# Windowed attention ahead of two mixture-of-experts layers: order of exponential and transpositions, layout of v, quarters of the array

## The chip, the cores and the metric

The kernel runs on one core of a Trainium2 chip. The metric is device microseconds of one execution. Beside the plain executions there is one taken with the profiler; its time and its span are given below.

## What is computed

Attention over q, k and v of shape (4, 8, 576, 64) with a window of 32 keys: heads 0 to 3 look at the last 32 positions, heads 4 to 7 at every fourth of the last 128. Its output, 2304 rows of 512, goes through a layer that assigns each row to one of 8 experts, with a capacity, and then through one that mixes two experts for each row.

```python
rel = pos[:, None] - pos[None, :]
mask_plain = (rel >= 0) & (rel < 32)
mask_dil = (rel >= 0) & (rel < 128) & (rel % 4 == 0)
scores = np.where(masks, scale * np.matmul(q, k.transpose(0, 1, 3, 2)), -1e9)
attn = np.exp(scores - scores.max(-1, keepdims=True))
x = np.matmul(attn / (attn.sum(-1, keepdims=True) + 1e-9), v)
x = moe(x)    # each row to one expert of 8, capacity N // 8
out = moe2(x) # two experts for each row, softmax over the two
```

## The kernel before

All data are float32. The host reorders the positions of the dilated heads so that they too become a plain window; then every block of 64 queries needs 96 keys. A group g is a batch and half of its heads (four heads, as two pairs i of two heads h); there are eight groups, and each is cut into a unit of five blocks and one of four, so 16 units u. Even groups hold the plain heads, odd groups the dilated ones.

For a unit, `scores` (L237) multiplies each block's queries with its 96 keys: 64 rows of the array for head h, 64 columns, output s in PSUM; VectorE scales and masks (L251) into p and takes the maximum (L256); GpSimd subtracts it (L257). `norm` (L259) has ScalarE take the exponential (L262), VectorE sum it (L264), add 1e-9 (L265) and invert (L266), and GpSimd multiply (L267). `flip` (L269) transposes p on TensorE (L278), four blocks to a PSUM tile ps, of which there are two, and ScalarE copies each tile out (sb, L280): three tiles for a unit of five blocks (4, 4 and 2 transpositions), two for one of four. `pv` (L286) multiplies with v (L297), and ScalarE copies the output o to x (L302, L308).

Each engine carries out its instructions in the order in which the program issues them. The loop at the end of `attention` issues for unit u: `flip(u)`, `norm(u + 2)`, `scores(u + 4)`, `pv(u)`; behind an even group come `gate` and `logits` of the batch before. So while a unit is transposed, VectorE and GpSimd work on later ones. Tiles of p are six, of s and o two each, of q, k and v four groups.

SP issues all loads on one queue, in the order of the calls of `load` (L217: q, k, and for the first two groups a half of the mask) and `load_v` (L226), with the constants ct and ct2 in between; groups 4 to 7 are issued as units finish. An issue waits until the DMA that last used its semaphore has landed; eight semaphores are used in turn. `consts2` (L176) makes small tables on GpSimd out of ct and ct2, issued behind the scores of unit 3. `warm` (L361) keeps TensorE busy with matmuls on zeros at the start. Attention ends with `steps` (L338, at 100.55 us in the trace) and the routing of the first expert layer follows.

Of the kernel before, what the change touches and what calls it, by code (L numbers as in the profile page):

```python
# [9 lines left out]
F32 = mybir.dt.float32  # L10
# [13 lines left out]
NT = N // 128  # L24
# [34 lines left out]
for _n, _w in (("ident", 128), ("iota", 128), ("prio", E), ("iota8", E),  # L59
               ("ge", 3 * NT), ("ge2", 5 * NCOL), ("pos", NCOL), ("ovf", (N - CAP2) // 128),  # L60
               ("tri", 128), ("shift", (len(DIGITS) + len(DIGITS_FIX)) * NT), ("tri1", 128), ("tokcp", NT * 2), ("colp", NCOL * 2)):
    if _n == "tri":
        _WK = _W
    _C[_n] = (_W, _w)
    _W += _w


def _constants():
# [8 lines left out]
    put("ident", np.eye(128))  # L77
    put("tri", (p[:, None] < p[None, :]))
    put("iota", p)
# [36 lines left out]
def prep(inputs):  # L116
# [10 lines left out]
    y[:, :, 4:] = x[:, :, 4:].reshape(B, 144, 4, 4, D).transpose(0, 2, 1, 3, 4).reshape(B, S, 4, D)  # L127
    a["v"] = y.reshape(B, S, DM)
    g = np.zeros((4, 128, 32), np.float32)
# [16 lines left out]
class Body:  # L146
# [29 lines left out]
    def consts2(self):  # L176
        nc, c, cp = self.nc, self.c, self.cp
        self.tri = cp.tile([128, 128], BF, name="tri")
        nc.gpsimd.tensor_copy(self.tri, c("tri"))
        self.ones = cp.tile([128, 128], BF, name="ones")  # L180
        nc.gpsimd.memset(self.ones, 1.0)
        self.iotab = cp.tile([128, 128], BF, name="iotab")
        nc.gpsimd.tensor_copy(self.iotab, c("iota"))
        self.c256 = cp.tile([128, 128], BF, name="c256")
        nc.gpsimd.memset(self.c256, 256.0)
        self.shift = cp.tile([128, self.nr, NT], I32, name="shift")
        o = 0 if self.exact else len(DIGITS) * NT
        nc.gpsimd.tensor_copy(self.shift.rearrange("p r c -> p (r c)"), c("shift")[:, o:o + self.nr * NT])
        self.tri1 = cp.tile([128, 128], BF, name="tri1")
        nc.gpsimd.tensor_copy(self.tri1, c("tri1"))  # L190
        self.prio = cp.tile([128, E], BF, name="prio")
        nc.gpsimd.tensor_copy(self.prio, c("prio"))
        self.tokcp = cp.tile([128, NT, 2], BF, name="tokcp")
        nc.gpsimd.tensor_copy(self.tokcp.rearrange("p c v -> p (c v)"), c("tokcp"))
        self.pt4 = self.st.tile([GB, NCOL, 4], BF, name="pt4")
        nc.gpsimd.tensor_copy(self.pt4[:, :, 0:2], c("colp", GB).rearrange("p (c v) -> p c v", v=2))
        self.L = self.st.tile([128, NT, E], F32, name="L")
        self.unit = self.st.tile([128, 1], F32, name="unit")


    def attention(self, x0T):
        nc, tc, A = self.nc, self.tc, self.A
        with ExitStack() as ctx:
# [22 lines left out]
            def load_v(g):  # L226
                b, t = divmod(g, 2)
                VT[g] = vp.tile([KW, NB, 256], F32, name="vt")
                v = A["v"]
                nc.sync.dma_start(VT[g][:, 0, :], v[b, 0:KW, 256 * t:256 * t + 256])  # L230
                nc.sync.dma_start(VT[g][:, 1:NB, :],
                                  bass.AP(tensor=v.tensor, offset=v.offset + (b * S + 32) * DM + 256 * t,
                                          ap=[[DM, KW], [64 * DM, NB - 1], [1, 256]]))

            groups = [(g, j0, n) for g in range(2 * B) for j0, n in (CUTS if g == 0 else ((0, 5), (5, 4)))]

            def scores(u):  # L237
                g, j0, n = groups[u]
                s = pS.tile([128, 2, 512], F32, name="s")
                for i in range(2):  # L240
                    for jj in range(n):
                        j = j0 + jj
                        w = _win(j)
                        for h in range(2):
                            r = slice(64 * h, 64 * h + 64)
                            nc.tensor.matmul(s[r, i, jj * KW:(jj + 1) * KW], QT[g][r, i, 64 * j:64 * j + 64],  # L246
                                             KT[g][r, i, w:w + KW], start=True, stop=True)
# [21 lines left out]
            def flip(u):  # L269
# [4 lines left out]
                while q < 2 * n:  # L274
# [8 lines left out]
                    q += m  # L283
                return blk

            def pv(u, blk):  # L286
                g, j0, n = groups[u]
                b, t = divmod(g, 2)
                for i in range(2):
                    o = pO.tile([128, 512], F32, name="o")  # L290
                    for jj in range(n):
                        sb, a = blk[i * n + jj]
                        j = j0 + jj
                        for h in range(2):
                            r = slice(64 * h, 64 * h + 64)
                            hh = 2 * i + h
                            nc.tensor.matmul(o[r, jj * 64:(jj + 1) * 64], VT[g][:, j, hh * 64:hh * 64 + 64],  # L297
                                             sb[:, a, r], start=True, stop=True)
                    dst = x0T[2 * t + i][:, b * S:(b + 1) * S]
# [77 lines left out]
            load_v(3)  # L377
            nu = len(groups)
            scores(0)
            scores(1)  # L380
# [4 lines left out]
            scores(3)  # L385
            self.consts2()
            warm(WARM[2])
            for u, (g, j0, n) in enumerate(groups):
                if j0 == 0 and g + 4 < 2 * B:
                    load(g + 4)  # L390
                    load_v(g + 4)
                blk = flip(u)
                if u + 2 < nu:
                    norm(u + 2)
                if u < len(WARM) - 3:
                    warm(WARM[3 + u])
                if u + 4 < nu:
                    scores(u + 4)
                pv(u, blk)
                if g and g % 2 == 0:  # L400
                    if j0 == 0:
# [1070 lines left out]
```

## Time and profile before

| | |
|---|---|
| median of three executions | 919.64 us (917.78 to 921.02) |
| profiled execution | 921.74 us |
| its span, first to last instruction | 919.9 us |
| TensorE busy | 851.6 us (93%) |
| VectorE busy | 517.9 us (56%) |
| ScalarE busy | 367.1 us (40%) |
| GpSimd busy | 183.8 us (20%) |
| instruction fetches (DMA queue q8) | 55 packets, 0.90 MB |

Busy time is that of the whole span, in which attention is the first ninth; what bounds that stretch is read from the stretch itself. PE is TensorE, DVE VectorE, ACT ScalarE, POOL GpSimd, SP SyncE; L12 is line 12 of the kernel before.

### The profile page before, as it was taken

Reading aid. Unit: us, or ns where it says so; the run is one execution under the profiler, and the core shown is the slowest. Engines: PE = TensorE matmul, PEld = TensorE weight load, DVE = VectorE, ACT = ScalarE, POOL = GpSimd, SP = SyncE. Lnnn points to the kernel's source line nnn. Section 1 sums busy time; section 2 is a strip of 40 time slices with the busy share of each in tenths; the row PEclk is TensorE's granted clock in tenths of the full one; section 3 lists DMA queues with packets and bytes.
Section 4 is the critical chain, followed back from the end, with each engine's and each line's share of the span. In section 5 each row is a group of like instructions: output and inputs, shape, how many; then the busy total and the mean of one; then the engine's idle time right before and its main releaser. Section 6 shows DMA issues by size and latency. Waiting matters only on the chain.

```text
span 919.9 us, 16944 instructions
## 1 busy us (share of the span) xinstructions
PE 851.6 (93%) x6723; PEld 772.8 (84%) x6725; DVE 517.9 (56%) x1540; ACT 367.1 (40%) x669; POOL 183.8 (20%) x155
## 2 busy tenths in 40 slices
PE   7789849889999999889898999999999999999993
PEld 5677738789988999789797989989899898998983
DVE  6557576779998643964855635427255272552300
ACT  2557643434334645545324334333343333432310
POOL 4646210110112100010023221221212212122011
PEclk9889969999999999999999999999999999999997
DMA  9962373436565765354335553544535445453012
GB/s 307 265 179 45 128 243 138 144 119 209 164 205 147 262 198 177 95 178 145 107 57 170 144 133 73 157 83 136 144 75 151 91 125 150 81 149 47 14 24 38
DMA packets 59641, 126.33 MB, mean 137 GB/s; under 512 B 7456, under 2 KB 14880, under 8 KB 59552
## 3 DMA queue, kind: packets, MB, share of 16 engines
q1 hardware_dynamic: 46080, 94.53, 33.0%
q0 software_dynamic: 10496, 25.77, 14.4%
q10 hardware_dynamic: 2976, 4.85, 1.7%
q8 instruction: 55, 0.90, 0.4%
q14 instruction: 34, 0.28, 0.1%
HBM read 100.49 MB, written 24.72 MB: 136 GB/s over the span
## 4 chain that ended last, share of the span: by engine, by line
PE 71%; DVE 13%; DMA 7%; ACT 4%; issue 3%; SPq 1%; POOL 1%; ACTq 0%; POOLq 0%; DVEq 0%
PE m L774 58%; DVE wlo L739 3%; PE s L246 2%; PE t L1048 2%; PE r L546 1%; DMA kt<-in_k_dram 1%; PE o L297 1%; DMA raw<-in_w2a_dram 1%; DMA g<-xr,idx 1%; DVE hl L762 1%; PE ps L278 1%; DVE R L683 1%; ACT whi L735 1%; DMA ct<-in_consts_dram 1%; PE t L434 1%
## 5 line engine op out<-in xcount | busy, mean ns | idle before, releaser
L774 PE MATMUL m<-xh,whi 128*128 128x384 f32 (+2 forms) x768 | 237.0, 309 | 0.6 <-DVE hl L762 0.6
L774 PE MATMUL m<-xl,whi 128*128 128x384 f32 (+2 forms) x768 | 236.1, 307 | 0.0
L774 PE MATMUL m<-xh,wlo 128*128 128x384 f32 (+2 forms) x768 | 235.9, 307 | 0.0
L739 DVE TENSOR_TENSOR wlo<-raw,whi 128x512 fp32r<-128x512 f32 x256 | 163.8, 684 | 52.2 <-ACT whi L735 51.9
L762 DVE SCALAR_TENSOR_TENSOR hl<-m,hh 128x256 fp32r<-128x256 f32 (+2 forms) x192 | 90.0, 476 | 151.5 <-ACT hh L761 135.2
L761 ACT ACTIVATE hh<-m 128x256 fp32r<-128x256 f32 (+2 forms) x192 | 81.3, 427 | 178.0 <-PE m L774 164.5
L774 PEld LDWEIGHTS m<-xl,whi 128*128 128x128 f32 x768 | 146.1, 190 | 4.7 <-issue 4.4
L735 ACT ACTIVATE whi<-raw 128x1024 fp32r<-128x1024 f32 x128 | 134.4, 1052 | 38.1 <-DMA raw<-in_w1a_dram 16.3
L774 PEld LDWEIGHTS m<-xh,whi 128*128 128x128 f32 x768 | 146.0, 190 | 1.2 <-DVE hl L762 0.8
L774 PEld LDWEIGHTS m<-xh,wlo 128*128 128x128 f32 x768 | 145.8, 190 | 0.5 <-issue 0.5
L774 PE MATMUL m<-whi,hl 128*128 128x512 f32 x320 | 129.0, 403 | 0.5 <-DVE hl L762 0.5
L774 PE MATMUL m<-wlo,hh 128*128 128x512 f32 x320 | 125.4, 392 | 0.0
L774 PE MATMUL m<-whi,hh 128*128 128x512 f32 x320 | 125.2, 391 | 0.0
L1085 POOL DMA_INDIRECT out_dram<-y,tk x40 | 64.1, 1604 | 278.7 <-ACT y L1084 264.5
L1084 ACT ACTIVATE y<-m,wte 128x512 f32<-128x512 f32 x40 | 27.5, 688 | 144.5 <-issue 93.9
L774 PE MATMUL m<-hh,whi 128*128 128x288 f32 x256 | 78.5, 307 | 3.6 <-DVE over L499 3.0
L758 DVE TENSOR_TENSOR xl<-t,xh 128x512 fp32r<-128x512 f32 (+1 forms) x72 | 41.8, 586 | 71.0 <-ACT xh L757 70.5
L774 PE MATMUL m<-hl,whi 128*128 128x288 f32 x256 | 79.3, 310 | 2.6 <-DVE hl L762 1.4
L774 PE MATMUL m<-hh,wlo 128*128 128x288 f32 x256 | 78.2, 306 | 0.0
L1034 POOL DMA_INDIRECT g<-x,pos x40 | 38.8, 970 | 177.9 <-issue 125.5
L774 PEld LDWEIGHTS m<-whi,hl 128*128 128x128 f32 x320 | 60.5, 189 | 12.5 <-DVE hl L762 1.4
L774 PEld LDWEIGHTS m<-wlo,hh 128*128 128x128 f32 x320 | 60.4, 189 | 12.6
(220 smaller groups left out, 1096.2 us busy)
## 6 DMA issues: line engine op xcount, KB each, us to landing
raw<-in_w1a_dram SPq DMA_DIRECT2D x32, 512.0 KB
raw<-in_w2a_dram SPq DMA_DIRECT2D x32, 512.0 KB
raw<-in_w1b_dram SPq DMA_DIRECT2D x32, 512.0 KB
raw<-in_w2b_dram SPq DMA_DIRECT2D x32, 512.0 KB
vt<-in_v_dram SPq DMA_DIRECT2D x8, 768.0 KB
qt<-in_q_dram SPq DMA_DIRECT2D x8, 576.0 KB
kt<-in_k_dram SPq DMA_DIRECT2D x8, 576.0 KB
xr<-g SPq DMA_DIRECT2D x18, 256.0 KB
```

What stands on the lines that cost most here:

```text
L246: nc.tensor.matmul(s[r, i, jj * KW:(jj + 1) * KW], QT[g][r, i, 64 * j:64 * j + 64], KT[g][r, i, w:w + KW], start=True, stop=True)
L278: nc.tensor.transpose(ps[:, a, :], p[:, q + a, :], self.ident)
L735: nc.scalar.activation(hi, raw, AF.Copy)
L739: self.pend.append((chunk, self.pe + LOW[0], lambda s=s: nc.vector.tensor_tensor(lo[:, s], raw[:, s], hi[:, s].bitcast(F32), op=OP.subtract)))
L758: self.nc.vector.tensor_tensor(xl, ps, xh.bitcast(F32), op=OP.subtract)
L761: self.nc.scalar.activation(hh, ps, AF.Relu)
L762: self.later(0.4, lambda: self.nc.vector.scalar_tensor_tensor(hl, ps, 0.0, hh.bitcast(F32), op0=OP.max, op1=OP.subtract))
L774: self.nc.tensor.matmul(ps, a, b, start=i == 0, stop=i == n - 1)
L1034: nc.gpsimd.indirect_dma_start(out=g[:, :DM], out_offset=None, in_=self.x1[:rows, :], in_offset=bass.IndirectOffsetOnAxis(ap=pos[:, b:b + ...
L1048: nc.tensor.transpose(ps[:, kk * 128:(kk + 1) * 128], g[:, kk * 128:(kk + 1) * 128], self.ident)
L1084: nc.scalar.activation(y, ps, AF.Copy, scale=wt[:, b:b + 1])
L1085: nc.gpsimd.indirect_dma_start(out=self.out, out_offset=bass.IndirectOffsetOnAxis(ap=tok[:, b:b + 1], axis=0), in_=y, in_offset=None, comp ...
```

## The change

Four things change. The scores' loop runs over block, pair i, head h, and the half of the output rows is h xor i, so that four matmuls in turn use all four combinations of row half and column half of the array; `pv` reads the halves accordingly. In the main loop `norm(u + 2)` is issued ahead of `flip(u)`, and `flip` hands back after its second tile, so that the third tile's transpositions stand behind `scores(u + 4)`. The host lays v out as [batch, half of heads, 64, 9 blocks, 256], so that a partition's eight blocks are one run of 8 KB, and `load_v` makes four DMAs of it instead of two. The unused table tri goes; `consts2` is issued ahead of the first scores, and five of its casts form `consts3`, issued behind `pv` of unit 6.

```diff
@@ load_v
-                v = A["v"]
-                nc.sync.dma_start(VT[g][:, 0, :], v[b, 0:KW, 256 * t:256 * t + 256])
-                nc.sync.dma_start(VT[g][:, 1:NB, :],
-                                  bass.AP(tensor=v.tensor, offset=v.offset + (b * S + 32) * DM + 256 * t,
-                                          ap=[[DM, KW], [64 * DM, NB - 1], [1, 256]]))
+                v = A["v"][b, t]
+                nc.sync.dma_start(VT[g][:64, 0, :], v[:, 0, :])
+                nc.sync.dma_start(VT[g][64:, 0, :], v[:KW - 64, 1, :])
+                nc.sync.dma_start(VT[g][KW - 64:, 1:, :], v[:, 1:, :])
+                nc.sync.dma_start(VT[g][:KW - 64, 1:, :], v[32:, :NB - 1, :])
@@ scores
-                for i in range(2):
-                    for jj in range(n):
-                        j = j0 + jj
-                        w = _win(j)
+                for jj in range(n):
+                    j = j0 + jj
+                    w = _win(j)
+                    for i in range(2):
                         for h in range(2):
                             r = slice(64 * h, 64 * h + 64)
-                            nc.tensor.matmul(s[r, i, jj * KW:(jj + 1) * KW], QT[g][r, i, 64 * j:64 * j + 64],
+                            nc.tensor.matmul(s[half(h ^ i), i, jj * KW:(jj + 1) * KW], QT[g][r, i, 64 * j:64 * j + 64],
                                              KT[g][r, i, w:w + KW], start=True, stop=True)
@@ flip
-                return blk
+                    yield blk
@@ pv
-                                             sb[:, a, r], start=True, stop=True)
+                                             sb[:, a, half(h ^ i)], start=True, stop=True)
@@ attention, ahead of the units
+            self.consts2()
             scores(0)
             scores(1)
             norm(0)
...
             scores(3)
-            self.consts2()
             warm(WARM[2])
             for u, (g, j0, n) in enumerate(groups):
...
-                blk = flip(u)
                 if u + 2 < nu:
                     norm(u + 2)
+
+                turn = flip(u)
+                next(turn)
+                blk = next(turn)
                 if u < len(WARM) - 3:
                     warm(WARM[3 + u])
                 if u + 4 < nu:
                     scores(u + 4)
+                for _ in turn:
+                    pass
                 pv(u, blk)
+                if u == 6:
+                    self.consts3()
```

On ScalarE, around unit 2, the program before has the two output copies of unit 1 (x_75, x_76), the three tile copies of unit 2 (sb), the exponential of unit 4 (p, 128x960) and the output copies of unit 2:

```order
L302 ACTIVATE x_75<-o 128x256
L302 ACTIVATE x_76<-o 128x256
L280 ACTIVATE sb<-ps 96x512 x2
L280 ACTIVATE sb<-ps 96x256
L262 ACTIVATE p<-p 128x960
L308 ACTIVATE x_77<-o 128x144 x2
```

The changed program has there:

```order
L307 ACTIVATE x_75<-o 128x256
L307 ACTIVATE x_76<-o 128x256
L267 ACTIVATE p<-p 128x960
L285 ACTIVATE sb<-ps 96x512 x2
L285 ACTIVATE sb<-ps 96x256
L313 ACTIVATE x_77<-o 128x144 x2
```

The exponential of unit 4 now stands ahead of the three copies of unit 2.

On GpSimd, at the start of the program, the first work on scores (p from p and the maxima mx) stands before right behind one memset:

```order
L325 MEMSET amo 128x128
L257 ISA
L257 TENSOR_TENSOR p<-p,mx 128x960
L257 TENSOR_TENSOR p<-p,mx 128x768
L267 TENSOR_TENSOR p<-p,su 128x960
```

And in the changed program:

```order
L330 MEMSET amo 128x128
L179 MEMSET ones 128x128
L181 CAST iotab<-ct 128x128
L183 MEMSET c_183 128x128
L262 ISA
L262 TENSOR_TENSOR p<-p,mx 128x960
L262 TENSOR_TENSOR p<-p,mx 128x768
```

Two memsets and a cast that reads ct, the constants that SP loads behind the first two groups' q, k and masks, have moved ahead of the first subtraction.

On SP, from the load of ct2 (ct_108) to q and k of group 3 (qt, kt), the program before issues v of groups 1 and 2 in two DMAs each:

```order
L373 DMA ct_108<-in_consts_dram 128x484
L230 DMA vt<-in_v_dram 96x256
L231 DMA vt<-in_v_dram 96x8x256
L230 DMA vt<-in_v_dram 96x256
L231 DMA vt<-in_v_dram 96x8x256
L220 DMA qt<-in_q_dram 128x2x576
L222 DMA kt<-in_k_dram 128x2x576
```

And the changed program:

```order
L378 DMA ct_108<-in_consts_dram 128x356
L231 DMA vt<-in_v_dram 64x256
L232 DMA vt<-in_v_dram 32x256
L233 DMA vt<-in_v_dram 64x2048
L234 DMA vt<-in_v_dram 32x2048
L231 DMA vt<-in_v_dram 64x256
L232 DMA vt<-in_v_dram 32x256
L233 DMA vt<-in_v_dram 64x2048
L234 DMA vt<-in_v_dram 32x2048
L221 DMA qt<-in_q_dram 128x2x576
L223 DMA kt<-in_k_dram 128x2x576
```

Each v is now four DMAs, two of them with runs of 2048 elements, and ct2 is narrower by the 128 columns of tri.

## Rows read from the trace of the kernel before

**Rows 1.** Windows of attention: stretch, length, each engine's busy us (instructions), clock, DMA

```profile
33.70:59.90 26.20, 21.14 (x335) 17.77 (x336) 12.72 (x20) 11.04 (x26) 11.86 (x8) 0.80 0.83 195
59.90:87.04 27.14, 26.07 (x509) 22.22 (x507) 19.42 (x29) 18.86 (x45) 17.20 (x11) 1.00 0.45 114
```

**Rows 2.** TensorE in order of time: start, length, work, count, idle before

```profile
33.71 1.87 PE L246 MATMUL s<-kt,qt 64*64 64x96 f32 x40 [2.54 <-DMA kt<-in_k_dram]
...
42.07 0.86 PE L297 MATMUL o<-sb,vt 96*64 96x64 f32 x18 [2.09 <-issue]
...
50.02 0.51 PE L278 MATMUL ps<-ct,p 128*96 128x128 f32 x3
53.35 1.30 PE L278 MATMUL ps<-ct,p 128*96 128x128 f32 x5 [2.83 <-issue]
```

**Rows 3.** DMA queues, 39 to 42 us (packets, MB, share of 16 engines)

```profile
q8 instruction: 1, 0.02, 2.8%
```

**Rows 4.** DMA queues, 50 to 52 us

```profile
q8 instruction: 1, 0.02, 4.0%
```

**Rows 5.** Busy time and granted clock after the two stops

```profile
42.07:46.00 3.93, 3.93 (x38) 3.08 (x39) 0.60 (x1) 2.92 (x8) 1.81 (x2) 0.57 1.07 258
53.35:59.90 6.55, 6.55 (x74) 5.83 (x75) 3.19 (x5) 2.68 (x5) 1.75 (x2) 0.52 0.10 36
```

**Rows 6.** VectorE in order of time, unit 6 to unit 8

```profile
64.67 1.09 DVE L251 SCALAR_TENSOR_TENSOR p<-s,mask 128x960 f32<-128x960 f32 x1
...
67.28 0.95 DVE L264 TENSOR_REDUCE su<-p 128x8 f32<-128x768 f32 x1 [0.26 <-ACT p L262]
68.27 0.71 DVE L265 TENSOR_SCALAR su<-su 128x8 f32<-128x8 f32 x1
...
69.14 0.91 DVE L251 SCALAR_TENSOR_TENSOR p<-s,mask 128x768 f32<-128x768 f32 x1
...
73.00 1.09 DVE L251 SCALAR_TENSOR_TENSOR p<-s,mask 128x960 f32<-128x960 f32 x1
```

**Rows 7.** GpSimd in order of time, the same stretch

```profile
67.16 1.79 POOL L257 TENSOR_TENSOR p<-p,mx 128x960 f32<-128x960 f32 x1 [0.48 <-DVE mx L256]
...
71.25 1.47 POOL L257 TENSOR_TENSOR p<-p,mx 128x768 f32<-128x768 f32 x1 [0.41 <-DVE mx L256]
```

**Rows 8.** VectorE in order of time, other units

```profile
15.48 1.11 DVE L251 SCALAR_TENSOR_TENSOR p<-s,mask 128x960 f32<-128x960 f32 x1
...
35.62 1.16 DVE L251 SCALAR_TENSOR_TENSOR p<-s,mask 128x960 f32<-128x960 f32 x1 [1.44 <-PE s L246]
...
81.84 1.15 DVE L264 TENSOR_REDUCE su<-p 128x10 f32<-128x960 f32 x1 [1.29 <-ACT p L262]
...
87.83 0.91 DVE L251 SCALAR_TENSOR_TENSOR p<-s,mask 128x768 f32<-128x768 f32 x1
...
93.96 0.95 DVE L264 TENSOR_REDUCE su<-p 128x8 f32<-128x768 f32 x1 [2.10 <-ACT p L262]
```

**Rows 9.** Chain of waits in order of time (start, us, what), one unit

```profile
61.66 1.80 PE s L246 x40
63.46 1.31 PE o L297 x40
64.77 1.01 PE ps L278 x8
```

**Rows 10.** DMA rate in three stretches (windows, last column GB/s)

```profile
4.00:10.00 6.00, 5.44 (x80) 3.84 (x80) 1.29 (x2) 0.00 (x0) 0.00 (x0) 1.00 1.05 411
20.00:24.00 4.00, 2.81 (x44) 2.62 (x46) 3.54 (x6) 0.68 (x1) 3.67 (x7) 0.76 1.10 246
122.50:127.00 4.50, 1.28 (x18) 1.29 (x19) 4.01 (x21) 2.12 (x2) 3.21 (x3) 0.50 1.00 381
```

**Rows 11.** Chain of waits, the load of the constants

```profile
4.57 8.10 DMA ct<-in_consts_dram
```

**Rows 12.** GpSimd in order of time, its first work on scores

```profile
11.10 3.31 POOL L257 TENSOR_TENSOR p<-p,mx 128x960 f32<-128x960 f32 x2 [10.15 <-DVE mx L256]
```

More of the change, by code (lines that the diff above doesn't have):

```diff
@@ L60 @@
                ("ge", 3 * NT), ("ge2", 5 * NCOL), ("pos", NCOL), ("ovf", (N - CAP2) // 128),
-               ("tri", 128), ("shift", (len(DIGITS) + len(DIGITS_FIX)) * NT), ("tri1", 128), ("tokcp", NT * 2), ("colp", NCOL * 2)):
-    if _n == "tri":
+               ("shift", (len(DIGITS) + len(DIGITS_FIX)) * NT), ("tri1", 128), ("tokcp", NT * 2), ("colp", NCOL * 2)):
+    if _n == "shift":
         _WK = _W
@@ L77, in _constants @@
     put("ident", np.eye(128))
-    put("tri", (p[:, None] < p[None, :]))
     put("iota", p)
@@ L127, in prep @@
     y[:, :, 4:] = x[:, :, 4:].reshape(B, 144, 4, 4, D).transpose(0, 2, 1, 3, 4).reshape(B, S, 4, D)
-    a["v"] = y.reshape(B, S, DM)
+    a["v"] = y.reshape(B, NB, 64, 2, 256).transpose(0, 3, 2, 1, 4)
     g = np.zeros((4, 128, 32), np.float32)
@@ L177, in consts2 @@
         nc, c, cp = self.nc, self.c, self.cp
-        self.tri = cp.tile([128, 128], BF, name="tri")
-        nc.gpsimd.tensor_copy(self.tri, c("tri"))
         self.ones = cp.tile([128, 128], BF, name="ones")
@@ L185, in consts2, with consts3 @@
         nc.gpsimd.memset(self.c256, 256.0)
+        self.L = self.st.tile([128, NT, E], F32, name="L")
+        self.unit = self.st.tile([128, 1], F32, name="unit")
+    def consts3(self):
+        nc, c, cp = self.nc, self.c, self.cp
         self.shift = cp.tile([128, self.nr, NT], I32, name="shift")
@@ L196, in consts2 @@
         nc.gpsimd.tensor_copy(self.pt4[:, :, 0:2], c("colp", GB).rearrange("p (c v) -> p c v", v=2))
-        self.L = self.st.tile([128, NT, E], F32, name="L")
-        self.unit = self.st.tile([128, 1], F32, name="unit")
     def attention(self, x0T):
@@ L228, in load_v, with half @@
                 VT[g] = vp.tile([KW, NB, 256], F32, name="vt")
-                v = A["v"]
-                nc.sync.dma_start(VT[g][:, 0, :], v[b, 0:KW, 256 * t:256 * t + 256])
-                nc.sync.dma_start(VT[g][:, 1:NB, :],
-                                  bass.AP(tensor=v.tensor, offset=v.offset + (b * S + 32) * DM + 256 * t,
-                                          ap=[[DM, KW], [64 * DM, NB - 1], [1, 256]]))
+                v = A["v"][b, t]
[3 more added lines that the diff above has]
+                nc.sync.dma_start(VT[g][:KW - 64, 1:, :], v[32:, :NB - 1, :])
             groups = [(g, j0, n) for g in range(2 * B) for j0, n in (CUTS if g == 0 else ((0, 5), (5, 4)))]
+            def half(c):
+                return slice(64 * c, 64 * c + 64)
             def scores(u):
```

## Prediction

> **What bounds the kernel now.** I read the windows first, then TensorE and VectorE in order of time, then the DMA queues. The change touches attention alone, the first 100.6 us of the span of 919.9 us. A "unit" is one pass of scores to output for five or four blocks of 64 queries; there are 16, and stt(u) is VectorE's L251 of unit u, the instruction that takes the scores of unit u out of PSUM.
>
> The windows show two different stretches [rows 1]: from 59.9 to 87.0 us TensorE is busy 26.07 of 27.14 us at clock 1.00, from 33.7 to 59.9 only 21.14 of 26.20 us at 0.80. In the second of these TensorE stands still twice, 2.09 us before 42.07 and 2.83 us before 53.35, and the reader sees "issue" as the cause: no semaphore was late [rows 2]. Between the two stops lie 127 matmuls and as many weight loads (18+10+40+40+16+3 by that view), 254 instructions; 254 counted back from the first stop, near 39.98, end just behind 33.71. In each stop one packet of the instruction queue moves 0.02 MB while the data queues are full [rows 3, 4]. So I read both stops as waits for the next piece of TensorE's own program, asked for when the piece before it was entered: at about 33.8 and at 42.07, come 8.3 and 11.3 us later, where TensorE needs a piece every 6 to 8 us. After each stop the granted clock is half, 0.57 and 0.52 [rows 5].
>
> The stretch from 59.9 looks TensorE-bound, but VectorE and GpSimd run in a closed loop there. From stt(10) at 64.67 to stt(11) at 69.14 are 4.47 us [rows 6]: L251 and L256, then GpSimd's L257 starts at 67.16 and ends at 68.95 [rows 7]; VectorE's tiny L265 starts at 68.27 and is stretched from its usual 0.17 us to 0.71, ending as L257 ends; 0.19 us later stt(11) starts. The next step is 3.86 us, and its L257 runs 71.25 to 72.72; with no wait for ScalarE it would end 0.19 behind that, at 72.91, so 3.77 us. The loop's floor for two units is 8.24 us, and it took 8.33.
>
> [...]
>
> **The change part by part.**
>
> *Scores in four quarters.* 40 matmul instructions of five blocks take 1.80 us, 45 ns each, the output's take 1.31 us, 33 ns each [rows 9]. Before, two quarters of the array work at a time. The trace shows no four: from below, nothing is gained (1.80 us); from above, half (0.90 us); the nearest row, the output's 33 ns, gives 1.32. I take 1.0 to 1.3. TensorE's pair of units then needs 7.9 us less about 1.3 (two times 1.0 for transposes, 1.31 + 1.05, 1.80 + 1.47, with 0.25 for the odd two): 6.6, under the loop's 8.24. So this edit frees TensorE, and the end moves only where TensorE is late: after a stop.
>
> *Exponential first, last transpositions behind the scores.* VectorE's L264 waits for ScalarE's exponential 1.29 us at 81.84 and 2.10 us at 93.96 [rows 8]. These go, down to the loop: five steps from stt(10) at 64.67 to stt(15) at 87.83 took 23.16 us; by the loop three of 4.47, two of 3.77 and a reduction of 0.38 are 21.33. **Gain 1.4 us** of at most 1.8 (from below 0.3, if copies behind the gate still delay ScalarE). Behind stt(15) the 2.10 us shrink to what GpSimd leaves; **0.9 us**, between 0 and 2.1. The price is that the copies of a unit start one exponential (0.84 to 1.0 us) later; the scores and the loop cover it.
>
> *v in 8 KB pieces.* While v moves alone the DMA engines are full at 246 GB/s; q, k and masks at the start reach 411, weights in 4 KB pieces 381 [rows 10]. A group's v is 0.885 MB: 3.6 us at 246, 2.3 at 381. Four DMAs instead of two, some to 64 or 32 partitions; no row shows 8 KB pieces, so 2.3 to 3.6, and I take 2.7. Three such groups lie ahead of the k that ends the wait at 33.71: it comes at about 31.0 (29.8 to 33.7). SP issues 16 more DMAs; with eight semaphores in turn fewer bytes are under way at once, but each wait has a group's data ahead of it, which covers it.
>
> *Constants.* Five casts move to unit 6 and one goes: GpSimd has idle time there, nothing. But GpSimd's cast of iota now stands ahead of the first L257, and it needs the constants, which land at 4.57 + 8.10 = 12.67 us [rows 11]; the first L257 started at 11.10 [rows 12]. It now starts near 13.2: 2.1 us late. Behind it are everything on GpSimd, the exponentials, and stt(2), which moves from 15.48 to 17.6 [rows 8]. By the loop stt(3) to stt(6) follow at 22.1, 25.8, 30.3 and 34.1. Before, stt(6) was at 35.62, waiting for scores and so for that k [rows 8]. So of 2.7 us by which k is early 1.5 remain. If k is no earlier, 0 to 0.8 remain; if the cast costs nothing, 3.5.
>
> *The stops.* From stt(6) to stt(10) are 64.67 - 35.62 = 29.05 us; the loop needs 16.48 and a reduction of 0.3: 12.2 us lie in the stops and the slow clock behind them. After: the piece asked for at about 31.2 comes, after 8.3 us, at 39.5, where TensorE needs it near 37; scores of unit 8 are then done by 42.2, and the loop wants them at 34.1 + 8.24 = 42.3. The first stop costs nothing. The second piece is asked for at 39.5 and needed at 45.0. With 11.3 us as before it comes at 50.8; with no crowd, in time. The load stream is some 5 us shorter by then (six groups at 0.9), so I take the middle, 48. From resumption to stt(10) it took 11.32 us, 6.55 of them at half clock; by the loop alone about 6; I take 8.7, so stt(10) at 56.7. That is **8.0 us** earlier, the first 1.5 included. The ends: 50.8 + 11.3 = 62.1, gain 2.6; no second stop, 1.5 + 12.2 = 13.7.
>
> **Sum:** 8.0 + 1.4 + 0.9 = 10.3 us. The profiled execution took 921.74 us: 911.4. It is 2.1 above the median of the three runs, 919.64, so for the median 909.3, say 909. What follows attention is the same instructions in the same order, and moves as a whole.
>
> **The rivals.**
>
> *The stops stay or grow* (0.22). A row in favour: the pieces took 8.3 and 11.3 us only while data queues were full, and full they stay. With latencies as before and v hardly faster: 2.6 + 0.3 + 0.2, about 916.5. [...] Against: loads are given out only as units finish, so a stopped TensorE lets the stream run dry. [...]
>
> *TensorE was the bound after all* (0.08). If L265 slips out of GpSimd's way, two units cost VectorE's 7.3 us and stt(10) to stt(15) gain some 3 us more: 904 to 906, and without stops 901.
>
> *Slower: v gets slower in its new pieces* (0.08). A transfer to 32 or 64 partitions may not keep all DMA engines busy. Each microsecond more for a group's v delays that k by 3 and the end of the stream by 6. At 0.6 us more (210 GB/s) the gains at the stops are used up, and it decides from there; at 1.5 us more (174 GB/s) k lands at 38.2, stt(6) is 3.7 us late, the stops stay: 924 to 927. For it: more and smaller DMAs. Against: 381 GB/s with 4 KB pieces.
>
> *The quarters do not run together*: no rival of its own; 7.9 us for two units stay under 8.24, and only the work behind a stop is 1 us longer: 910.
>
> **Numbers.** The forecast, 904 to 913, has 0.58; the stops' rival 0.22 (half of it within 0.3%), the earlier bound 0.08, the slower v 0.08, the rest 0.04. A measurement of this kernel tells about 0.3%, 2.8 us, from no change. Faster 0.81, same 0.10, slower 0.09. The range from 902.5 to 917 leaves out the slow side, part of the stops' rival and the best case.
>
> **What would show it.** Right: first L257 near 13.2; the scores that wait for k near 31; a TensorE stop by "issue" in unit 3 that the loop hides, a shorter one in unit 5; stt(10) near 57; steps of 4.47 and 3.77 us with L265 ending as GpSimd ends; attention's last output near 90. Wrong: packets of v at 246 GB/s or less; scores still 1.80 us; stops longer than 3 us or a third; two units in under 8 us; a half clock where TensorE now waits for the loop.

## The result, and the profile after

The changed kernel takes 910.59 us (median of five executions, 908.89 to 911.30) against 919.64 us of the kernel before (five, 915.14 to 921.02). The ratio is 0.9906, with a 95% interval of 0.9880 to 0.9932: faster by 9 us or 0.9%, by more than the 0.3% that can be told from no change. The profiled execution took 908.89 us with a span of 907.0 us. So the two profiles differ by 12.9 us and the medians by 9.05: the profile of before lies 2.1 us above its median, that of the changed kernel is its fastest execution. Behind attention nothing moved between these two: from attention's end (the start of `steps`, at 87.45 us now) to the end of the span it is 819.55 us after and 919.9 - 100.55 = 819.35 before. Over all the profiles of this study the same stretch took 817.3 to 822.6 us, so below it is attention's own times that are compared, and not the total of one profile.

The windows of the changed kernel, with columns as in [rows 1], cut at the takings of scores stt(6), stt(10) and stt(15), with the clock of the stretches around them:

```profile
33.69:50.16 16.47, 13.66 (x302) 10.63 (x300) 14.87 (x22) 11.15 (x26) 13.05 (x8) 1.00 1.02 297
50.16:73.59 23.43, 20.24 (x458) 16.64 (x459) 18.55 (x28) 16.71 (x44) 17.49 (x15) 1.00 0.48 122
73.59:87.45 13.86, 11.30 (x201) 8.76 (x198) 8.13 (x12) 11.19 (x30) 8.75 (x9) 1.00 0.01 2
24.00:38.01 14.01, 10.38 (x253) 8.68 (x247) 13.45 (x17) 8.81 (x21) 11.49 (x7) 1.00 1.03 309
38.01:104.00 65.99, 58.74 (x1058) 47.00 (x1059) 46.48 (x94) 47.54 (x110) 35.78 (x30) 1.00 0.51 152
```

From stt(6) to stt(10) it took 29.05 us before and takes 16.47 now, which is the loop's 16.48. VectorE is busy 14.87 us of it; TensorE has room. The granted clock is 1.00 from 24 us on, where [rows 5] showed 0.57 and 0.52.

TensorE in order of time, same columns as [rows 2]:

```profile
30.18 1.21 PE L251 MATMUL s<-kt,qt 64*64 64x96 f32 x40 [1.18 <-DVE su L271]
...
35.10 0.62 PE L302 MATMUL o<-sb,vt 96*64 96x64 f32 x13 [0.16 <-ACT sb L285]
38.01 0.80 PE L302 MATMUL o<-sb,vt 96*64 96x64 f32 x19 [2.29 <-issue]
...
39.75 1.06 PE L251 MATMUL s<-kt,qt 64*64 64x96 f32 x40
...
49.66 0.33 PE L302 MATMUL o<-sb,vt 96*64 96x64 f32 x2
51.33 1.38 PE L302 MATMUL o<-sb,vt 96*64 96x64 f32 x38 [1.34 <-issue]
...
56.79 0.40 PE L251 MATMUL s<-kt,qt 64*64 64x96 f32 x8
58.53 0.89 PE L251 MATMUL s<-kt,qt 64*64 64x96 f32 x32 [1.34 <-issue]
...
64.41 0.38 PE L251 MATMUL s<-kt,qt 64*64 64x96 f32 x3 [0.22 <-issue]
...
75.39 0.43 PE L283 MATMUL ps<-ct,p 128*96 128x128 f32 x2 [1.01 <-ACT sb L285]
...
79.98 1.17 PE L302 MATMUL o<-sb,vt 96*64 96x64 f32 x32 [0.55 <-ACT sb L285]
...
87.45 0.49 PE L343 MATMUL o<-amd,amo 128*128 128x128 f32 x2 [0.24 <-ACT x L313]
```

40 scores now take 1.06 us, 26 ns each; in the same view they took 1.87 us, 47 ns each [rows 2] (45 by [rows 9]). A transposition on 128 rows and 96 columns takes 126 ns for 128 columns of output [rows 9], so some 95 for the 96 of a score; 47 and 26 are a half and a little over a quarter of that, and that two and four quarters work at a time is an estimate from these times. The scores of unit 6 start at 30.18 instead of 33.71. The row names VectorE's L271 as what came last; but no tile leads from there to these scores, and a second profile of this kernel, below, names k, at 30.11. The first stop by "issue" is still there, inside unit 3's output; the second came in the middle of unit 5's transpositions before. There is none there now; smaller ones come further on in the program, of 1.34 us in unit 6's output, 1.34 us in the scores issued in unit 8, and 0.22 us 127 matmuls behind that. Behind 75 us TensorE waits for ScalarE's copies.

VectorE in order of time (L256, L269, L270 are L251, L264, L265 of before):

```profile
17.60 1.10 DVE L256 SCALAR_TENSOR_TENSOR p<-s,mask 128x960 f32<-128x960 f32 x1
...
33.69 1.09 DVE L256 SCALAR_TENSOR_TENSOR p<-s,mask 128x960 f32<-128x960 f32 x1
...
36.93 1.07 DVE L270 TENSOR_SCALAR su<-su 128x8 f32<-128x8 f32 x1
...
38.16 0.91 DVE L256 SCALAR_TENSOR_TENSOR p<-s,mask 128x768 f32<-128x768 f32 x1
...
41.93 1.10 DVE L256 SCALAR_TENSOR_TENSOR p<-s,mask 128x960 f32<-128x960 f32 x1
...
50.16 1.10 DVE L256 SCALAR_TENSOR_TENSOR p<-s,mask 128x960 f32<-128x960 f32 x1
...
54.18 0.95 DVE L269 TENSOR_REDUCE su<-p 128x8 f32<-128x768 f32 x1 [1.66 <-ACT p L267]
...
63.43 0.95 DVE L269 TENSOR_REDUCE su<-p 128x8 f32<-128x768 f32 x1 [1.54 <-ACT p L267]
...
73.59 0.91 DVE L256 SCALAR_TENSOR_TENSOR p<-s,mask 128x768 f32<-128x768 f32 x1
...
79.48 0.95 DVE L269 TENSOR_REDUCE su<-p 128x8 f32<-128x768 f32 x1 [2.03 <-ACT p L267]
```

GpSimd in order of time:

```profile
12.73 0.29 POOL L181 CAST iotab<-ct 128x128 bf16<-128x128 f32 x1 [11.65 <-DMA ct<-in_consts_dram]
...
13.22 3.21 POOL L262 TENSOR_TENSOR p<-p,mx 128x960 f32<-128x960 f32 x2
...
36.19 1.79 POOL L262 TENSOR_TENSOR p<-p,mx 128x960 f32<-128x960 f32 x1 [0.47 <-DVE mx L261]
```

The steps 33.69, 38.16, 41.93 are the loop's 4.47 and 3.77 to the hundredth. The addition at 36.93 on eight numbers per row takes 1.07 us and ends at 38.00, GpSimd's subtraction at 36.19 + 1.79 = 37.98. And GpSimd's first subtraction starts at 13.22, behind the cast that waited for the constants.

### The profile page after: what moved, and what is told of

It is laid out like the page before. It is cut to its first block, busy times and chain, and to the rows that moved or that the text cites. A ratio compares the mean times of both kernels' runs of the same rounds, so it can differ in the third digit from the quotient of the medians.

```text
span 907.0 us, 16969 instructions
## 1 busy us (share of the span) xinstructions
PE 838.4 (92%) x6723; PEld 760.1 (84%) x6725; DVE 518.9 (57%) x1540; ACT 366.7 (40%) x669; POOL 183.6 (20%) x154
## 4 chain that ended last, share of the span: by engine, by line
PE 72%; DVE 14%; DMA 5%; issue 3%; ACT 3%; POOL 1%; ACTq 0%; SPq 0%; POOLq 0%; DVEq 0%
PE m L786 60%; DVE wlo L751 3%; PE o L302 2%; PE t L1060 2%; PE r L558 2%; PE ps L283 1%; DMA g<-xr,idx 1%; DVE hl L774 1%; DVE R L695 1%; DMA raw<-in_w2a_dram 1%; DMA ct<-in_consts_dram 1%; PE t L810 1%; PE t L446 1%; PE s L251 1%; PE t L848 1%
```

## The experiments

**Theory** (that of the prediction): VectorE and GpSimd run in a closed loop of 8.24 us for two units; what lies above it is lost at the late k and at the stops, which are waits for TensorE's program while the data queues are full. **Rivals**: TensorE itself was the bound, and the faster scores gave the gain; the order of the exponential gave it; the stops belong to something in the data, not to places in the program.

Ratios are against the kernel before, run beside each; diffs are against the changed kernel, but for the two runs that put one part into the kernel before.

**The loads of v as before, the rest changed.**

```diff
-    a["v"] = y.reshape(B, NB, 64, 2, 256).transpose(0, 3, 2, 1, 4)
+    a["v"] = y.reshape(B, S, DM)
@@ load_v: the two DMAs of the kernel before instead of the four
```

> The changed kernel with v loaded as before (two DMAs in 1 KB pieces). Loop and fetch theory: the k that unit 6's scores need lands near 33 instead of 30, TensorE's program comes later, the first stop ends near 41 instead of 38.0 and the later ones grow; stt(10) moves from 50.2 to 54 to 58, the whole is 3 to 8 us slower than the changed kernel. Rival (faster scores are the gain): within 1 us of the changed kernel.

Measured 913.82 us, ratio 0.9949 (0.9928 to 0.9971); stt(10) at 53.49, just below the range expected, and attention's end at 92.86, against 87.45. TensorE again stands still ahead of unit 6's scores (row from TensorE in order of time):

```profile
33.37 1.88 PE L251 MATMUL s<-kt,qt 64*64 64x96 f32 x40 [4.65 <-DVE su L270]
```

It names VectorE again, which had just ended; that it is k that came late, the run with the old v below shows, whose row names k at 33.84. In the window from 32 us the clock is half:

```profile
32.00:40.00 8.00, 6.63 (x98) 5.68 (x102) 4.09 (x6) 2.91 (x9) 4.81 (x3) 0.57 1.08 263
```

TensorE passes the place of the first stop late and without a stop; the next two are 1.53 us up to 54.84 and 2.30 up to 63.02. By the medians the run takes 3.2 us more than the changed kernel, by the ratios 4, and the intervals just touch: that is what the layout of v is worth beside the rest.

**The quarters as before.**

```diff
-                for jj in range(n):
...
-                    for i in range(2):
+                for i in range(2):
+                    for jj in range(n):
...
-                            nc.tensor.matmul(s[half(h ^ i), i, jj * KW:(jj + 1) * KW], ...
+                            nc.tensor.matmul(s[r, i, jj * KW:(jj + 1) * KW], ...
-                                             sb[:, a, half(h ^ i)], ...
+                                             sb[:, a, r], ...
```

> The changed kernel with the scores' loop and halves as before (two quarters at a time). Loop theory: scores take 1.80 us again, TensorE's pair of units 7.9 us stays under the loop's 8.24; the end moves by 0 to 2 us, most of it behind the stops. Rival (TensorE is the bound): 0.74 + 0.58 us for every pair of units, 8 us and more slower.

Measured 910.25 us, 0.9916 (0.9893 to 0.9940), scores 1.87 us again, stt(10) at 52.05, attention's end at 89.36. That is 1.9 us later than in the changed kernel's profile and 3.9 later than in its second one, below, but the times can't be told apart: scores that take half the time are worth a small part of the 9 us at most. As the source of the gain the rival "TensorE was the bound" falls. But in this run TensorE is the bound: it is busy 9.85, 10.00 and 9.85 us in the three stretches of 10 us from 40 to 70, and VectorE waits for its scores. The middle one of these stretches, and VectorE's takings stt(10) and stt(14):

```profile
50.00:60.00 10.00, 10.00 (x205) 8.84 (x203) 8.27 (x12) 7.16 (x19) 8.42 (x10) 1.00 0.76 235
...
52.05 1.16 DVE L256 SCALAR_TENSOR_TENSOR p<-s,mask 128x960 f32<-128x960 f32 x1 [0.43 <-PE s L251]
...
70.08 1.16 DVE L256 SCALAR_TENSOR_TENSOR p<-s,mask 128x960 f32<-128x960 f32 x1 [0.56 <-PE s L251]
```

These four units take 18.03 us, where the loop needs 16.48. Before, with the old order too, they took 18.70, from stt(10) at 64.67 [rows 6] to stt(14):

```profile
83.37 1.10 DVE L251 SCALAR_TENSOR_TENSOR p<-s,mask 128x960 f32<-128x960 f32 x1
```

The slower TensorE meets its program almost in time: only two stops are left, of 0.79 us up to 31.48 and 0.62 up to 38.34.

**The order as before.**

```diff
+                for blk in flip(u):
+                    pass
                 if u + 2 < nu:
                     norm(u + 2)
-                turn = flip(u)
-                next(turn)
-                blk = next(turn)
...
-                for _ in turn:
-                    pass
```

> The changed kernel with the exponential of unit u+2 issued behind unit u's transpositions again, all three tiles of transpositions ahead of the scores. Loop theory: VectorE waits for exponentials some 0.4 to 1.6 us a unit again, 1 to 4 us slower up to stt(15), and about 1 us won back behind it, where no scores cover the copies that wait for an exponential: in all 0 to 3 us slower. Rival (the order is what the loop needed): 5 us or more slower.

Measured 909.23 us, 0.9908 (0.9883 to 0.9932). The profile shows two effects that cancel. stt(10) comes at 55.07, 4.9 us later than with the new order: the first stop is 2.98 us there, the exponentials stand behind the copies that TensorE delivers late, and VectorE waits for them:

```profile
42.01 1.16 DVE L269 TENSOR_REDUCE su<-p 128x10 f32<-128x960 f32 x1 [2.05 <-ACT p L267]
...
49.34 0.95 DVE L269 TENSOR_REDUCE su<-p 128x8 f32<-128x768 f32 x1 [3.46 <-ACT p L267]
```

From stt(10) to attention's end at 88.88 it then takes 33.81 us, against 37.29 in the changed kernel, so 3.5 us are given back: 1.3 before stt(15) at 77.19, where the stops by "issue" are only 0.31 and 0.48 us, and 2.2 behind it. What the new order brings is that the loop runs on across a stop; at attention's end it costs.

**The tables behind unit 3's scores, as before.**

```diff
-            self.consts2()
             scores(0)
...
             scores(3)
+            self.consts2()
```

> The changed kernel with the small tables of GpSimd issued behind the scores of unit 3 again, so that GpSimd does not wait for the constants first. Loop theory: the first subtraction starts near 10.2 instead of 13.2, stt(2) near 14.7 instead of 17.6, stt(6) near 31 (its k lands at 30) instead of 33.7, and the first stop gives part of it back: 1 to 2.5 us faster than the changed kernel. Rival (the start is covered by the loads): no difference behind stt(6).

Measured 907.61 us, 0.9886 (0.9859 to 0.9913). The first subtraction starts at 10.17, stt(2) is at 14.55 instead of 17.60 and stt(6) at 31.50 instead of 33.69. The stop in unit 3's output is 1.01 us; then TensorE stops elsewhere, 2.01 us, 127 matmuls further on (one missing in the view), and stt(10) is late, at 52.11:

```profile
44.82 1.52 PE L283 MATMUL ps<-ct,p 128*96 128x128 f32 x7 [2.01 <-issue]
```

A loop that is 2.2 us ahead runs into the next piece. Attention ends at 86.88, which lies between the two profiles of the changed kernel (87.45 and, below, 85.48). The cast's cost at the start is shown, its worth in the time isn't: the intervals overlap.

**Twenty matmuls on zeros more ahead of the units.**

```diff
-WARM = (14, 2, 9)
+WARM = (14, 2, 29)
```

> The changed kernel with 20 more matmuls on zeros ahead of the first transpositions, where TensorE waits 5.3 us anyway; nothing else is moved, TensorE's program is 40 instructions longer there. If the stops are waits for the next piece of TensorE's program, each moves 20 matmuls up: from the output of unit 3, 13 matmul rows in, to the scores of unit 7, some 25 of 32 rows in; from the output of unit 6 (2 rows in) into the scores of unit 10, some 24 of 40 rows in. If they belong to the work (a load, a semaphore), they stay at the same instructions. Time within 2 us of the changed kernel.

One execution, 908.47 us. TensorE in order of time:

```profile
41.88 0.33 PE L302 MATMUL o<-sb,vt 96*64 96x64 f32 x3 [0.87 <-issue]
...
47.89 0.72 PE L251 MATMUL s<-kt,qt 64*64 64x96 f32 x24
50.75 0.56 PE L251 MATMUL s<-kt,qt 64*64 64x96 f32 x16 [2.13 <-issue]
...
54.96 1.10 PE L302 MATMUL o<-sb,vt 96*64 96x64 f32 x29 [0.15 <-ACT sb L285]
58.14 0.33 PE L302 MATMUL o<-sb,vt 96*64 96x64 f32 x3 [2.08 <-issue]
```

The stops moved back along the program. The one that stood 2 rows into unit 6's output now stands in the scores ahead of it, 24 rows in: 16 + 2 + 2 = 20 rows earlier. The one that stood 8 rows into the scores of unit 12 now stands 3 rows from the end of unit 7's output: 3 + 8 + 8 = 19 rows earlier, where a missing record can account for the one. Between the three stops stand 127 matmuls each time, as between the two of [rows 2]. The stop is in the program, not in the data.

**VectorE's addition left out.** Left out is the 1e-9 that is added to the sums, which are at least 1, so that in float32 it changes none of them.

```diff
-                nc.vector.tensor_scalar(su[:, :2 * n], su[:, :2 * n], 1e-9, None, op0=OP.add)
```

> The changed kernel without VectorE's addition of 1e-9 to the sums (each sum is at least 1, so in float32 the addition changes nothing). Loop theory: nothing on VectorE waits for GpSimd's subtraction; the steps of two units fall from 8.2 us to some 7.0 to 7.3, where VectorE and GpSimd are each nearly full; stt(10) 2 to 4 us earlier, 3 to 6 us faster in all unless stops for the program take it. Rival (TensorE or the stops are the bound): under 1 us.

Measured 906.09 us, 0.9868 (0.9846 to 0.9890). VectorE's takings of scores, unit 2 to 5:

```profile
17.36 1.10 DVE L256 SCALAR_TENSOR_TENSOR p<-s,mask 128x960 f32<-128x960 f32 x1
...
20.66 0.91 DVE L256 SCALAR_TENSOR_TENSOR p<-s,mask 128x768 f32<-128x768 f32 x1
...
23.91 1.09 DVE L256 SCALAR_TENSOR_TENSOR p<-s,mask 128x960 f32<-128x960 f32 x1
...
27.27 0.91 DVE L256 SCALAR_TENSOR_TENSOR p<-s,mask 128x768 f32<-128x768 f32 x1
```

A step takes 3.25 to 3.36 us in place of 4.47 and 3.77, with one instruction of 0.17 us gone. GpSimd runs almost without a gap there (the longest is 0.22 us); its 1.79 and 1.47 us are the step. Then the loads catch it (k ends a wait of 1.25 us at 30.01, and a stop of 0.67 follows within these scores), and the stop in unit 3's output, 2.21 us up to 38.46, is no longer hidden; a slower clock follows, in this window:

```profile
40.00:44.00 4.00, 4.00 (x78) 3.06 (x78) 2.67 (x4) 2.18 (x5) 1.69 (x1) 0.62 0.96 323
```

stt(10) is at 51.30, later than in the changed kernel and not earlier as expected, stt(15) at 70.89 and attention's end at 85.53. The interval still touches that of the changed kernel.

**The old order in units 12 and 13 alone**, where no scores are left to issue.

```diff
-                if u + 2 < nu:
+                if u + 4 < nu:
                     norm(u + 2)
...
                 for _ in turn:
                     pass
+                if u + 2 < nu <= u + 4:
+                    norm(u + 2)
```

> The changed kernel with the exponentials of units 14 and 15 issued behind the transpositions of units 12 and 13 again, where no scores are left to cover the copies. TensorE's waits for copies at 75.4 (1.01 us) and 80.0 (0.55 us) go or shrink to 0.3: 0.5 to 1.2 us faster. Rival (the tail is bound by VectorE and GpSimd): no difference, or slower by the exponentials' delay.

Measured 908.52 us, 0.9879 (0.9855 to 0.9903). From stt(15) to the end it took 13.23 us instead of 13.86, and TensorE's waits for copies shrank from 1.01 and 0.55 to 0.31 and 0.30. The 0.6 us can be seen in the profile, not in the time. The stop in unit 3's output is 3.11 us in this profile, up to 38.60, stt(10) is at 52.00 and attention's end at 88.24.

**The tables, the addition and the order of units 12 and 13 together**, the three diffs above.

> The three together: tables behind the scores of unit 3, no addition of 1e-9, old order in the last units. If the loop of VectorE and GpSimd bounds attention, the gains add up to 4 to 9 us below the changed kernel; if the stops for TensorE's program bound it, 1 to 3.

Measured 906.03 us, 0.9866 (0.9843 to 0.9888): no better than without the addition alone. TensorE now stops at five pieces in a row, for 1.86, 0.96, 0.53, 1.05 and 1.03 us up to 36.23, 43.28, 49.83, 56.75 and 63.45; a loop that runs faster waits for the program.

**The new layout of v alone, in the kernel before**, its host line and its four DMAs.

> The kernel before with the new layout and four DMAs of v alone. If the loads feed everything (k earlier, program pieces sooner), it holds half of the change or more: k of unit 6 near 30, 3 to 6 us faster than before. If the parts need each other (TensorE with the old scores and order again 7.9 to 8.3 us for two units behind every stop), under 2 us.

Measured 911.58 us, 0.9908 (0.9874 to 0.9942), beside 0.9897 of the changed kernel: by itself it has most of the gain, by the medians 7.0 us of 9.7. One stop of 0.84 us is left, up to 36.49; the clock is 1.00 from 24 to 60 us; stt(10) is at 52.33, attention's end at 88.20. From stt(10) to stt(14) it takes 18.70 us, as before, with TensorE never idle for more than 0.31 us.

**The rest alone**: quarters, order and the five later casts in the kernel before, v as it was, the other tables behind unit 3's scores.

> The kernel before with the new scores' loop and the new order alone: v as before, the tables of GpSimd at their old place. Loop and fetch theory: k of unit 6 at 33 to 34 as before, stt(6) near 35, the stops remain, but TensorE runs behind them at 6.6 us for two units and meets the loop sooner: 3 to 5 us faster than before. If the loads feed everything: under 2 us.

Measured 912.63 us, 0.9939 (0.9909 to 0.9968), with stt(10) at 54.56 and attention's end at 94.42. Both parts alone attack the same loss: stt(10) was at 64.67, the one brings 12.3 us, the other 10.1, both together 14.5. By the medians they bring 7.0 and 5.9 us, and together 9.7. The two runs also show how k comes earlier. From 12 us to the scores that k releases, first with the new v alone:

```profile
12.00:29.45 17.45, 13.26 (x221) 10.41 (x217) 15.81 (x21) 9.99 (x17) 14.65 (x18) 1.00 1.02 332
```

and with the rest alone:

```profile
12.00:33.84 21.84, 11.67 (x198) 8.93 (x189) 16.63 (x23) 9.39 (x16) 16.45 (x13) 0.81 1.09 281
```

The rate is 332 GB/s instead of 281, and k is there when 5.79 MB have moved (17.45 by 332), not 6.14 (21.84 by 281). Of the 4.4 us the rate makes 3.4 (6.14 MB at 332 take 18.5 us), the smaller amount 1.0. The rate is the surer part: counted in the same way, the two profiles of the changed kernel moved 5.76 and 5.94 MB, so one kernel's amounts differ by half as much.

**The changed kernel again**, unchanged, beside the last two.

> The changed kernel itself, beside the parts on one chip: 0.988 to 0.993 of the time before; if the parts add up, the gains of v alone and of the rest alone sum to its gain, if they overlap, to more.

Measured 908.82 us, 0.9897 (0.9861 to 0.9933); stops of 1.99, 1.14 and 0.21 us. Here k does end the wait, 3.6 us earlier than in [rows 2]; then stt(10), stt(15) and attention's end:

```profile
30.11 1.17 PE L251 MATMUL s<-kt,qt 64*64 64x96 f32 x40 [1.57 <-DMA kt<-in_k_dram]
...
49.71 1.10 DVE L256 SCALAR_TENSOR_TENSOR p<-s,mask 128x960 f32<-128x960 f32 x1
...
71.60 0.91 DVE L256 SCALAR_TENSOR_TENSOR p<-s,mask 128x768 f32<-128x768 f32 x1
...
85.48 0.49 PE L343 MATMUL o<-amd,amo 128*128 128x128 f32 x2 [0.24 <-ACT x L313]
```

From stt(10) to stt(15) it is 21.89 us here, 1.5 less than in the first profile of the same kernel; behind stt(15) it is 13.88, as there.

**The late loads left out.** Units of groups 4 to 7 compute on q, k and v of groups 0 to 3, so the second half of the output isn't the reference's.

```diff
+                if g >= 4:
+                    QT[g], KT[g] = QT[g - 4], KT[g - 4]
+                    return
...
+                if g >= 4:
+                    VT[g] = VT[g - 4]
+                    return
```

> The changed kernel without the loads of groups 4 to 7 (their units compute on the data of groups 0 to 3, so these outputs are those of other heads). If full data queues delay TensorE's program, all stops by issue over 0.5 us behind 36 us vanish, stt(10) to stt(15) falls from 23.4 us to some 21.6, and attention ends 1.5 to 4 us earlier. If a piece takes its time whatever the queues do, the stops stay where they are.

One execution, 907.33 us. No stop by "issue" is left between 28 and 86 us. VectorE's takings of scores, unit 10 to 12 (L262 there):

```profile
49.88 1.10 DVE L262 SCALAR_TENSOR_TENSOR p<-s,mask 128x960 f32<-128x960 f32 x1
54.35 0.91 DVE L262 SCALAR_TENSOR_TENSOR p<-s,mask 128x768 f32<-128x768 f32 x1
58.12 1.09 DVE L262 SCALAR_TENSOR_TENSOR p<-s,mask 128x960 f32<-128x960 f32 x1
```

The window from stt(10) to stt(15) and the next, to attention's end:

```profile
49.88:71.20 21.32, 18.71 (x422) 15.08 (x420) 20.46 (x28) 16.19 (x41) 17.45 (x15) 1.00 0.01 3
71.20:86.06 14.86, 12.05 (x193) 8.90 (x193) 8.13 (x12) 10.78 (x28) 8.74 (x9) 0.89 0.01 2
```

With the queues empty the stops are gone, and the five steps take 21.32 us where the prediction worked out 21.33. But attention ends at 86.06, between the two profiles of the changed kernel and not 1.5 to 4 us earlier, for TensorE then waits 2.22 us for the copies behind the exponential, up to 72.59, and the clock is 0.89 in that window.

## Why the prediction was right, and where it missed

The time of 909.0 us was 1.6 below the median. The sum by the profiles was 10.3 us and came out as 12.9; by the medians, 9.05. Its terms did not come out alike, and that the time was met so closely is in part luck.

**Start and constants: right.** First subtraction 13.22 (predicted near 13.2), stt(2) 17.60 (17.6), stt(6) 33.69 (34.1). With the tables moved back stt(2) fell to 14.55, so the cast that waits for the constants is the cause.

**v in 8 KB pieces: right in kind, a little too small.** k came at 30.1, 3.6 us earlier; 2.7 were predicted, inside the bounds. I had worked it out from the rate of v alone; in the two runs with one part each the rate makes 3.4 us of 4.4, and the rest, 0.35 MB less ahead of that k, was not foreseen and is not well shown.

**Scores in four quarters: right in size, wrong in what they are for.** 1.06 us (1.0 to 1.3 predicted), and with the old quarters the time is the same within the intervals. But the step "TensorE's pair of units then needs 7.9 us", so that it stays under the loop's 8.24 even with the old scores, left out `gate` and `logits`: 1.18 and 0.66 to 0.80 us for every four units, by which TensorE's four units go above the loop's 16.48. With the old quarters and no stop they take 18.70 us (new v alone) and 18.03 (new order as well); with the new ones and no late loads 16.48, from 49.88 to 66.36. So the stretch from 59.9 us that "looks TensorE-bound" was bound by TensorE, and the faster scores are what lets the loop set the pace. In the time little of it is seen, because a faster TensorE reaches the next piece of its program before it is there: 5.2 us of stops in the changed kernel (3.3 in its second profile), 1.4 with the old quarters.

**The stops: right mechanism, mis-sized.** The first came where it was expected (2.29 us up to 38.01, predicted 39.5; 127 matmuls back from it lie near 30.4, 7.6 us before) and cost nothing: stt(8) at 41.93, predicted 42.3. The second was forecast to last until 48 with a half clock behind it and stt(10) at 56.7; stt(10) came at 50.16. So "8.0 us earlier" measured 14.5, above even the bound of 13.7. The step that failed is "I take the middle, 48": that piece came without any stop, at most 6.1 us behind 38.01, and the next three took 7.2, 7.2 and 5.9 (from the end of 127 matmuls at 44.1 to 51.33, to 58.53 and to 64.41), not 8.3 or 11.3. That a piece is asked for when the one before it is entered, and so all of these times, is an estimate from the counts; no row shows it. What the traces show is a packet of q8 ahead of the end of each stop of over 1 us, by 2.5 to 2.8 us: at 39.3 and 50.8 for 42.07 and 53.35 before, at 35.4, 48.7 and 56.0 for 38.01, 51.33 and 58.53 now. So the prediction's "in each stop one packet" is not right for its first stop, which began at 39.98. That the stops belong to the program's pieces and to full data queues is shown by the two runs that moved them, by 20 and 19 matmuls, and removed them. Between two stops lie 127 matmuls and as many weight loads, 254 instructions in the trace; while loads ran the stops lasted up to 3.11 us, and without the late loads none was left from 28 to 86 us.

**Two units in 8.24 us: right, and so shown.** The steps are 4.47 and 3.77 us in the changed kernel and in the run without late loads; without the addition they fall to 3.25 to 3.36. The addition ends with GpSimd's subtraction, at 38.00 behind 37.98 here and at 68.98 behind 68.95 before [rows 6, 7], and takes 1.07 and 0.71 us where it takes 0.17 by itself. What holds it no row shows.

**stt(10) to stt(15): wrong in the first profile, met in the second, and not for the reason given.** Predicted 1.4 us less; measured 23.43 against 23.16, 0.3 more, and 21.89, 1.3 less. The two differ in the stops that fall into this stretch, 1.34, 1.34 and 0.22 us against 1.14 and 0.21. In the first profile the waits for the exponential did not go; they are the stops passed on. At 54.18 the exponential stands on ScalarE behind unit 6's output copies, and those waited for the stop up to 51.33; at 63.43 it stands behind the copy of unit 8's third tile, which waited for the stop up to 58.53. Without the late loads the stretch is 21.32, the predicted 21.33, so the size was right but for stalls that the prediction had put earlier. The step "these go, down to the loop" failed: it credits the order, but with the new order and the old quarters, and no stop, the stretch is still 22.93 (52.05 to 74.98). Most of it hung on the scores.

**Behind stt(15): wrong.** Predicted 0.9 less, measured 13.86 (13.88 in the second profile) against 100.55 - 87.83 = 12.72, 1.1 more. The wait of 2.10 us for the exponential did not shrink; it is 2.03 at 79.48. The step that failed is "the scores and the loop cover it": in units 12 and 13 no scores follow, and TensorE waits for copies behind the exponential, 1.01 and 0.55 us. With the old order there 0.6 us of it come back. With the old order in all units the stretch is 11.69 us (77.19 to 88.88), but stt(15) itself comes 3.6 us later there, so how the rest divides stays open.

14.5 - 0.3 - 1.1 = 13.1 us is the span's 12.9 but for 0.2 behind attention; in the second profile attention ends 15.0 + 1.3 - 1.2 = 15.1 us earlier. A too careful 8.0 and a later part that brought less than forecast cancelled to a good sum.

**The rivals.** The stops stay or grow: no, by the same estimate the pieces took 7.6 us and less against 8.3 and 11.3; the half of its chance that is "within 0.3%" is for pieces of the program that come later beside larger data pieces, a term that no run shows. But a third stop came, which the prediction had named as a sign of being wrong, and in sum TensorE stands still for its program as long as before, 5.2 us against 4.9 (3.3 in the second profile); what changed is that the loop was fed ahead of the first, and that no half clock followed. TensorE the bound, with two units at VectorE's 7.3 us: no; with the addition in place two units take 7.98 and 8.11 us at the start (17.60 to 25.58 to 33.69) and 8.24 from there. No row or run shows the 7.3; without the addition two units took 6.55 and 6.61 us (17.36 to 23.91, 20.66 to 27.27). Slower v: no; with transfers to 64 and 32 partitions among them the loads ran at 309 GB/s with a DMA share of 1.03 (24.00 to 38.01).

## What to carry to other kernels

When every busy engine has room and a stall reads "issue", count instructions between two such stalls. An equal count, here 127 matmuls each time, pointed to a wait for the engine's program, and one run each tested it: 20 more dummies moved the stops back by 20 and 19 matmuls, and with the data queues empty none was left. Such a stall cost nothing here while the loop was fed from ahead of it, as at the first stop of 2.29 us, with stt(8) at 41.93, the loop's 8.24 behind stt(6); faster matmuls, 26 ns instead of 47, then met the next one sooner, 5.2 us of stops against 1.4 with the old quarters. Issue the pacing chain first, but look at the last passes, where the work that covered the new order is missing. When you add up an engine's time for a pass, count the work that comes only every few passes. Two edits that attack one loss did not add up: the new v alone gave 12.3 us at stt(10), the rest alone 10.1, both 14.5. And take a second profile before a stretch is called slower: 1.5 us lay between two of the same kernel.

## What the runs showed of the hardware that had not been expected

A stop does not always bring the half clock. Behind the 2.29 us of the changed kernel, the 1.99 of its second profile and 2.13 and 2.08 with more matmuls on zeros the granted clock stayed at 1.00. Behind 2.21 without the addition its mean fell to 0.62 (40 to 44), behind 2.01 with the tables moved back to 0.54 (44.82 to 48.00), behind 2.98 with the old order to 0.50 (40 to 44), behind 3.11 with the old order in units 12 and 13 to 0.59 (40 to 44), and behind the 2.09 before to 0.57 [rows 5]. In windows of 1 us the kernel before shows 1.00 from 33 to 42 us, 0.77 from 42, 0.50 from 43 to 45, 0.52 from 45 and 1.00 again from 46 to 52, so its 0.57 is a mean over both levels. So the length of the stop alone does not decide; what does stays open.

With v in 8 KB pieces the loads ran at 332 GB/s from 12 us to the k that releases unit 6 (the new v alone), and in 1 KB pieces at 281 (the rest alone). Whether less data also goes ahead of that k (5.79 against 6.14 MB) stays open: the profile doesn't show the 16 DMA engines one by one.

An addition to eight numbers per row, 0.17 us by itself, costs the loop 0.8 us a unit: 4.12 on the average of 4.47 and 3.77, against 3.3. The fastest kernels of the study leave it out (906.09 us, and 906.03 with two more edits); by the ratios that is some 3 us below the changed one, with intervals that touch. There the loop outruns the program's pieces, which stop TensorE five times in a row.
